# One table of small steps for the attention part, a shift taken off VectorE, and one-hot rows issued by SP alone

## The chip, the core and the metric

The kernel runs on one core of a Trainium2 chip. Five engines run side by side, each through its own list of instructions in order: TensorE (PE in the rows; PEld is its weight load), VectorE (DVE), ScalarE (ACT), GpSimd (POOL) and SyncE (SP). An instruction that has to wait holds up everything behind it on its engine; engines wait for each other through semaphores. SP and ACT also issue DMA transfers (SPq and ACTq in the rows). The metric is the device time of one execution in microseconds (us), as the median of several runs; lower is better.

## The reference

Three blocks in a row: attention restricted to clusters, a soft mixture of experts, and a feed-forward with `h - tanh(h)`.

```python
q_assign = np.argmax(np.einsum('bhsd,hcd->bhsc', q_n, c_n), axis=-1)   # 16 clusters
k_assign = np.argmax(np.einsum('bhsd,hcd->bhsc', k_n, c_n), axis=-1)
mask = q_assign[:, :, :, None] == k_assign[:, :, None, :]
scores = np.where(mask, scale * np.matmul(q, k.transpose(0, 1, 3, 2)), -1e9)
attn = softmax(scores)                      # B=4, H=8, S=768, D=64
x = (attn @ v).transpose(0, 2, 1, 3).reshape(3072, 512)
logits = x @ phi                            # 32 slots
slot_input = softmax_over_tokens(logits).T @ x
slot_out = relu(slot_input @ w1[e]) @ w2[e] # 8 experts, 4 slots each
x = softmax_over_slots(logits) @ slot_out
h = x @ w_in                                # 512 -> 2048; w_in, w_out are float64
out = (h - np.tanh(h)) @ w_out
```

## The kernel before

The attention part works on 16 **pairs** (batch, two heads), numbered p = 0 to 15. For each pair the steps are these functions:

- `load_raw`, `load_v`: q and k (768 KB) and v are loaded. `split_hi` (ScalarE) and `split_lo` (GpSimd) cut q and k into a coarse part and a rest; `xy_hi` and `xy_lo` copy these by DMA into the operand tile `xy`.
- `assign_mm`, `assign_t`, `assign_1` to `assign_6`: the cluster of each token, as one-hot rows. `xy_hot` copies the one-hot rows into `xy` by eight small DMAs, four issued by SP and four by ACT (all eight by SP for p = 0).
- `smax` (18 of them a pair): TensorE makes a row of scores in a PSUM tile `g` (four such tiles), VectorE reduces it to a row maximum `mx`. `sfin_1` to `sfin_4` turn the maxima into one row of `xy` for each head: VectorE, a transpose on TensorE, ScalarE, a DMA out to `row` in DRAM (issued by ACT) and a DMA back into `xy` (issued by SP).
- `st` (24 a pair): two matmuls make scores `st` (two PSUM tiles), ScalarE writes their exponential `E` (six tiles of two heads). `pvmm` (six a pair, kb = 0 to 5) multiplies E by v; GpSimd adds E into the sums `es`, whose single buffer is free again once `fin_sum` of that pair has read it.
- `fin_copy`, `fin_sum`, `fin_ss`, `fin_rec`, `fin_rcp`, `fin_x`, `fin_xm`: sums, division and projection of the pair. There is one `fin_sum` a pair, on TensorE, some six `st` after the pair's last one.
- After the fourth pair of each batch the `fl_` steps compute the batch's slot softmax; most of them are VectorE instructions.

Beside the pairs run 16 conversions of the float64 weights w_in and w_out to float32. Each loads 1 MB (`conv_load`), ScalarE scales the high words (`conv_1`), and VectorE makes the float32 bits from integer words in three passes (`conv_2` shift left, `conv_3` shift right and or, `conv_4` and and or); `conv_8` stores them, `conv_9` sums squares for w_in. `unit` loads 512 KB of expert weights into a buffer as soon as the attention part is done with it; 34 of 80 are issued inside the attention part.

The order in which a step's instructions enter the engine lists is set by a table `PLAN` of due positions: 24 positions are one pair, each step of pair p has one offset for all pairs (a few pairs have their own), all steps are sorted by position, and each step emits all its instructions for all engines at once. So a `smax` puts its matmuls into TensorE's list and its reduction into VectorE's list at the same place of the order, `pvmm` brings its GpSimd additions with it, and `xy_hi`, `xy_lo` and `xy_hot` each bring all their DMAs.

After the attention part come the expert block, paced by its weights, and the feed-forward, neither of which the change touches.

## Time and profile before

| | us |
|---|---|
| time, median of 3 runs | 869.48 |
| lowest and highest | 868.2 and 873.78 |
| the profiled execution, its own time | 873.71 |
| its span in the trace | 871.9 |

The attention part takes the first 514 us of the span, the expert block lasts to about 569 us, and the feed-forward fills the rest. The span is the time from the first to the last instruction; the difference to the execution's own time (1.8 us) is start and end of the program. "PEclk" in the rows is the clock that TensorE was granted, as a share of the full 2.4 GHz (the lower level is 1.2 GHz), averaged over the stretch. A matmul counts as busy also while it is still draining, so a busy TensorE need not be at its peak.

### The profile page before, as it was taken

The numbers are of one execution on the slowest core, as the hardware profiler recorded it, in microseconds if no ns is written. First come the engines' busy times: TensorE is split into PE (matmuls) and PEld (weight loads), VectorE is DVE, ScalarE is ACT, GpSimd is POOL, SyncE is SP. The second block draws the span as 40 slices with busy tenths as digits, with TensorE's granted clock in tenths as the row PEclk, the third lists the DMA queues.
The fourth block names the chain that finished last, engine by engine and source line by source line (L and its number), as shares of the span: only waits on it lengthen the run. The fifth ranks groups of instructions, "written<-read, shape, count | busy, mean of one in ns | idle before, by whom it ended". The sixth has DMA issues, their size and how long they took to land.

```text
span 871.9 us, 12716 instructions
## 1 busy us (share of the span) xinstructions
PE 806.9 (93%) x4327; PEld 541.6 (62%) x4327; DVE 617.7 (71%) x1033; ACT 500.6 (57%) x1069; POOL 403.5 (46%) x235
## 2 busy tenths in 40 slices
PE   1889988999999989999999979989999999999997
PEld 0545554665556556665556543358888888888886
DVE  3577575888768997879986571068767777677774
ACT  3344645565665565556544541179767767677673
POOL 2165975886888778888956741157000000000000
PEclk9988998999999999999999997989999999999999
DMA  6987597668657874777659589970100000000001
GB/s 172 240 217 181 175 215 205 165 175 203 175 164 196 205 191 134 207 197 183 187 156 343 200 320 406 392 292 1 38 25 13 36 1 37 37 0 37 1 38 39
DMA packets 49533, 135.13 MB, mean 155 GB/s; under 512 B 6866, under 2 KB 9350, under 8 KB 49460
## 3 DMA queue, kind: packets, MB, share of 16 engines
q1 hardware_dynamic: 40780, 114.81, 44.9%
q10 hardware_dynamic: 8680, 19.43, 7.2%
q8 instruction: 36, 0.59, 0.3%
q14 instruction: 37, 0.30, 0.1%
HBM read 78.55 MB, written 14.78 MB: 107 GB/s over the span
## 4 chain that ended last, share of the span: by engine, by line
PE 71%; DVE 9%; DMA 3%; ACT 1%; issue 1%; SPq 0%; ACTq 0%; DVEq 0%
PE pv L415 10%; PE acc L1027 10%; PE acc L1025 10%; PE acc L1026 10%; PE g L356 6%; PE st L404 6%; PE st L405 5%; PE u L966 3%; PE h L872 2%; DVE mx L361 2%; PE g L470 2%; PE o L891 2%; PE g L441 1%; DVE pgc L664 1%; DMA xy<-pgb 1%
## 5 line engine op out<-in xcount | busy, mean ns | idle before, releaser
L408 ACT ACTIVATE E<-st 128x384 f32<-128x384 f32 x384 | 168.2, 489 | 184.8 <-PE st L405 141.7
L424 POOL TENSOR_TENSOR es<-es,E 128x768 f32<-128x768 f32 x126 | 252.1, 2020 | 42.4 <-ACT E L408 37.0
L361 DVE TENSOR_REDUCE mx<-g 128x1 f32<-128x512 f32 (+1 forms) x288 | 187.5, 682 | 85.1 <-PE g L356 84.4
L415 PE MATMUL pv<-E,v 128*64 128x384 f32 x768 | 150.8, 513 | 1.9 <-DVE pvc L432 1.9
L1027 PE MATMUL acc<-whi,glo 128*128 128x512 f32 x384 | 150.7, 392 | 0.0
L1025 PE MATMUL acc<-whi,ghi 128*128 128x512 f32 x384 | 150.2, 391 | 0.0
L1026 PE MATMUL acc<-wlo,ghi 128*128 128x512 f32 x384 | 150.0, 391 | 0.0
L404 PE MATMUL st<-xy 112*128 112x384 f32 x384 | 140.8, 367 | 6.4 <-ACT E L408 6.4
L405 PE MATMUL st<-xy 97*128 97x384 f32 x384 | 130.9, 341 | 0.8 <-DMA xy<-row 0.8
L356 PE MATMUL g<-xy 112*128 112x512 f32 (+1 forms) x384 | 117.7, 386 | 9.9 <-DVE mx L361 3.7
L998 DVE TENSOR_TENSOR gt<-u,y 128x384 f32<-128x384 f32 x128 | 71.3, 557 | 50.9 <-ACT y L994 49.7
L356 PEld LDWEIGHTS g<-xy 112*128 112x128 f32 x384 | 67.0, 197 | 62.2 <-issue 16.7
L404 PEld LDWEIGHTS st<-xy 112*128 112x128 f32 x384 | 73.2, 191 | 48.5 <-issue 21.4
L994 ACT ACTIVATE y<-u 128x384 f32<-128x384 f32 x128 | 62.9, 492 | 57.5 <-PE u L966 56.6
L421 POOL TENSOR_TENSOR es<-E 128x768 f32<-128x768 f32 x32 | 58.2, 1841 | 60.3 <-PE g L441 60.3
L415 PEld LDWEIGHTS pv<-E,v 128*64 128x64 f32 x768 | 47.2, 139 | 62.0 <-issue 50.6
L1027 PEld LDWEIGHTS acc<-whi,glo 128*128 128x128 f32 x384 | 72.3, 188 | 17.8 <-DVE glo L1015 2.9
L1025 PEld LDWEIGHTS acc<-whi,ghi 128*128 128x128 f32 x384 | 72.7, 189 | 15.1
L1005 DVE SCALAR_TENSOR_TENSOR gt<-z,gt 128x384 f32<-128x384 f32 x128 | 72.1, 563 | 14.1 <-ACT ghi L1013 0.9
L996 ACT ACTIVATE z<-y,kt 128x384 f32<-128x384 f32 x128 | 79.2, 619 | 4.2
L1026 PEld LDWEIGHTS acc<-wlo,ghi 128*128 128x128 f32 x384 | 72.6, 189 | 10.4
L250 POOL TENSOR_TENSOR pgb<-pga 128x768 fp32r<-128x768 f32 x31 | 61.5, 1986 | 34.8 <-ACT pga L242 23.1
(149 smaller groups left out, 942.2 us busy)
## 6 DMA issues: line engine op xcount, KB each, us to landing
pgw<-in_w_dram SPq DMA_DIRECT2D x64, 512.0 KB
xy<-pga SPq DMA_DIRECT2D x15, 768.0 KB
pga<-in_qk_dram ACTq DMA_DIRECT2D x14, 768.0 KB
pgc<-in_w_in_dram SPq DMA_DIRECT2D x8, 1024.0 KB
pgc<-in_w_out_dram SPq DMA_DIRECT2D x8, 1024.0 KB
xy<-pga SPq DMA_DIRECT2D x18, 384.0 KB
xy<-pga SPq DMA_DIRECT2D x32, 192.0 KB
xy<-pgb SPq DMA_DIRECT2D x32, 192.0 KB
```

Source lines behind the costliest of these rows:

```text
L356: PE.matmul(g[:, o:o + kn], lhsT=x[0:112, QX, qt * 128:(qt + 1) * 128], rhs=x[0:112, KX, k0:k0 + kn], start=True, stop=True)
L361: DVE.tensor_reduce(out=m[:, m0:m0 + w], in_=g.rearrange("p (a b) -> p a b", a=w), axis=AX.X, op=ALU.max)
L404: PE.matmul(s, lhsT=x[0:112, KX, ks], rhs=x[0:112, QX, qs], start=True, stop=False)
L405: PE.matmul(s, lhsT=x[0:97, KY, ks], rhs=x[0:97, QY, qs], start=False, stop=True)
L408: ACT.activation(out=et[p, kb, c][:, h, :], in_=s, func=ACTF.Exp, scale=scale)
L415: PE.matmul(pv[p, c][64 * h:64 * h + 64, :], lhsT=vt[p][:, kb, h, :], rhs=et[p, kb, c][:, h, :], start=(kb == 0), stop=(kb == NKB - 1))
L424: eng.tensor_tensor(out=es[p][:, c], in0=es[p][:, c], in1=e, op=ALU.add)
L996: ACT.activation(out=z, in_=y, func=ACTF.Square, scale=POLY[0], bias=sq_b)
L1005: DVE.scalar_tensor_tensor(out=gt, in0=z, scalar=POLY[2], in1=gt, op0=ALU.add, op1=ALU.mult)
L1025: PE.matmul(acc[t], lhsT=a[:, ts], rhs=whi[:, f, :], start=(f == 0), stop=False)
L1026: PE.matmul(acc[t], lhsT=a[:, ts], rhs=wlo[:, f, :], start=False, stop=False)
L1027: PE.matmul(acc[t], lhsT=l[:, ts], rhs=whi[:, f, :], start=False, stop=(f == KF - 1))
```

## The change

- The table `PLAN` is replaced by `ORDER`. It gives each single step of each single pair its own place, and steps that use several engines are cut into parts with a place each: the matmuls of `smax` and its reduction, the matmuls of `st` and its exponential, the two halves of `fin_copy`, of `setup_2` and of some `fl_` steps. `xy_hi`, `xy_lo`, `xy_rest` and `xy_hot` are cut into single DMAs; the GpSimd additions leave `pvmm` and become steps `es_add`. Functions that have parts are generators, and the emission loop advances them.
- `conv_2`, the left shift on VectorE, is gone. ScalarE makes the low bits instead (`Identity` with a scale and a bias), and `conv_3` shifts left and ors in one VectorE pass. VectorE has two passes for each conversion instead of three, ScalarE two instead of one (three with the squares).
- All eight one-hot DMAs of a pair are issued by SP.

The diff, cut to its core:

```diff
-PLAN = {
-    "A": {
-        "raw": -11.3, "v": 27.0, "hi": [-6.3, -4.2], "lo": [-2.2, 0.1], "mm": 2.1, ...
+ORDER = {
...
+    "xy_hot": (
+        "0,0:26;0,1:27;0,2:25;0,3:23;0,4:57;0,5:30;0,6:35;0,7:33;1,0:116;...
...
     def split_lo(p, h):
-        if h == 0:
+        low(p)
+        (DVE if p == 0 and h == 0 else POOL).tensor_tensor(out=lo[p, h].bitcast(F32R), in0=raw[p, h], in1=hi[p, h], op=ALU.subtract)
...
-    def xy_hot(p):
-        tf = xy[p].bitcast(F32)
-        for h in range(2):
-            for c in range(2):
-                r = 64 * h + 32 * c
-                for a, e in ((QX, SP), (KX, ACT if p else SP)):
-                    e.dma_start(out=tf[96:96 + NC, a, h, c * HS:(c + 1) * HS], in_=oht[p][r:r + NC])
-                    r += NC
+    def xy_hot(p, j):
+        tf = scores(p)
+        h, c, k = j // 4, j // 2 % 2, j % 2
+        r = 64 * h + 32 * c + NC * k
+        SP.dma_start(out=tf[96:96 + NC, KX if k else QX, h, c * HS:(c + 1) * HS], in_=oht[p][r:r + NC])
...
             PE.matmul(g[:, o:o + kn], lhsT=x[0:112, QX, qt * 128:(qt + 1) * 128], rhs=x[0:112, KX, k0:k0 + kn], start=True, stop=True)
             o += kn
+        yield
...
-        for c in range(2):
-            e = et[p, kb, c]
-            if kb == 1:
...
+    def es_add(p, kb, c):
+        if p not in es:
+            es[p] = a1.tile([128, 2, 2, HS], F32, tag="es", name="es")
+        add_engine(p, kb, c).tensor_tensor(out=es[p][:, c], in0=et[p, 0, c] if kb == 1 else es[p][:, c], in1=et[p, kb, c], op=ALU.add)
...
     def conv_2(n):
+        _, lw, sg, _ = cv[n]
+        ACT.activation(out=sg.bitcast(U32), in_=lw.bitcast(U32), func=ACTF.Identity, scale=LO_SCALE, bias=lo_b)
+
+    def conv_3(n):
         hw, _, sg, _ = cv[n]
-        DVE.tensor_scalar(out=sg.bitcast(U32), in0=hw.bitcast(U32), scalar1=3, scalar2=None, op0=ALU.logical_shift_left)
-
-    def conv_3(n):
-        _, lw, sg, _ = cv[n]
         sg = sg.bitcast(U32)
-        DVE.scalar_tensor_tensor(out=sg, in0=lw.bitcast(U32), scalar=29, in1=sg, op0=ALU.logical_shift_right, op1=ALU.bitwise_or)
+        DVE.scalar_tensor_tensor(out=sg, in0=hw.bitcast(U32), scalar=3, in1=sg, op0=ALU.logical_shift_left, op1=ALU.bitwise_or)
...
-    for pos, i, f, a in sorted(ev, key=lambda e: e[:2]):
-        f(*a)
+    todo = sorted((at, k, n, a) for (n, a), ats in order_table().items() for k, at in enumerate(ats))
+    running = {}
+    for _, k, n, a in todo:
+        if k == 0:
+            running[n, a] = named[n](*a)
+        if running[n, a] is not None:
+            next(running[n, a])
```

What this does to the engine lists is seen at three places. The names are tiles: `st` scores, `g` a PSUM tile of `smax` (from `xy`) or of a `fin_` step, `pv` the result of `pvmm`. The line numbers of the two programs differ.

**TensorE, around `fin_sum` of pair 9 (`g<-es`), in the first third of pair 10.** Before:

```order
L356 MATMUL g_3572<-xy_3253 128x512
L415 MATMUL pv_3575<-E_3514,v_3230 64x384 x2
L415 MATMUL pv_3576<-E_3540,v_3230 64x384 x2
L404 MATMUL st_3590<-xy_2910 128x384
L405 MATMUL st_3590<-xy_2910 128x384
L404 MATMUL st_3595<-xy_2910 128x384
L405 MATMUL st_3595<-xy_2910 128x384
L441 MATMUL g_3601<-es_3339,kt_77 32x384 x4
L356 MATMUL g_3610<-xy_3253 128x512
L378 MATMUL g_3613<-kt_77,mxf_3599 6x128
```

After:

```order
L605 MATMUL g_3579<-xy_3149 128x512
L658 MATMUL st_3584<-xy_2848 128x384
L659 MATMUL st_3584<-xy_2848 128x384
L658 MATMUL st_3588<-xy_2848 128x384
L659 MATMUL st_3588<-xy_2848 128x384
L605 MATMUL g_3593<-xy_3149 128x512
L671 MATMUL pv_3596<-E_3503,v_3233 64x384 x2
L671 MATMUL pv_3597<-E_3554,v_3233 64x384 x2
L698 MATMUL g_3606<-es_3291,kt_77 32x384 x4
L671 MATMUL pv_3596<-E_3525,v_3233 64x384 x2
L671 MATMUL pv_3597<-E_3581,v_3233 64x384 x2
L630 MATMUL g_3629<-kt_77,mxf_3622 6x128
```

Before, one `pvmm` stands between every four `st`; now the `pvmm` of kb = 0 and 1 stand together after eight `st`, and so do the others, two by two.

**VectorE, in the first batch's `fl_` steps, from a pair's maximum row on.** (`mx` is a `smax` reduction, `mxf` is `sfin_1`, `xe` is `fin_xm`, `pgc` a conversion; `l`, `lg`, `rm` and `call` belong to the `fl_` steps.) Before:

```order
L366 TENSOR_REDUCE mxf<-mx 128x6
L659 SCALAR_TENSOR_TENSOR pgc<-pgc 128x2x512
L475 TENSOR_TENSOR xe<-g,rr 128x2x256 x2
L495 TENSOR_REDUCE l_1776<-xe 128x192
L497 TENSOR_TENSOR lg<-lg,l_1776 128x192
L505 TENSOR_REDUCE rm<-lg 128x6
L664 SCALAR_TENSOR_TENSOR pgc<-pgc 128x2x512
L361 TENSOR_REDUCE mx<-g 128x1
L509 TENSOR_TENSOR call<-lg,rm 128x192
```

After:

```order
L618 TENSOR_REDUCE mxf<-mx 128x6
L928 SCALAR_TENSOR_TENSOR pgc<-pgc 128x2x512
L732 TENSOR_TENSOR xe<-g,rr 128x2x256
L613 TENSOR_REDUCE mx<-g 128x1
L752 TENSOR_REDUCE l_1832<-xe 128x192
L613 TENSOR_REDUCE mx<-g 128x2
L613 TENSOR_REDUCE mx<-g 128x1 x4
L754 TENSOR_TENSOR lg<-lg,l_1832 128x192
L762 TENSOR_REDUCE rm<-lg 128x6
L688 TENSOR_TENSOR pvc<-pv,pvc 128x384 x2
```

Before, seven VectorE passes stood between two `smax` reductions, two of them conversion passes; now single reductions stand between the batch's steps, and the conversion pass `conv_4` (L928) is done ahead of them.

**SP, around the copies of pair 10's maximum rows (`xy<-row`).** (`xy<-pgb 16x384` are the one-hot rows, `pgc<-in_w_out_dram` a 1 MB `conv_load`, `w_out<-pgc` a `conv_8`.) Before:

```order
L643 DMA pgc<-in_w_out_dram 128x2x512
L320 DMA xy<-pgb 32x1536
L322 DMA xy<-pgb 32x1536
L323 DMA xy<-pgb 64x1536
L324 DMA xy<-onesrow 1x1536
L342 DMA xy<-pgb 16x384 x4
L396 DMA xy<-row 1x768 x2
L676 DMA w_out_75<-pgc 128x2x512
```

After:

```order
L907 DMA pgc<-in_w_out_dram 128x2x512
L594 DMA xy<-pgb 16x384 x7
L650 DMA xy<-row 1x768
L594 DMA xy<-pgb 16x384
L940 DMA w_out_75<-pgc 128x2x512
L907 DMA pgc<-in_w_out_dram 128x2x512
L650 DMA xy<-row 1x768
L562 DMA xy<-pga 64x2x1536
```

Before, both heads' rows followed four one-hot rows together; now the first head's row goes alone behind seven, and the second head's stands last, behind a store and a 1 MB load. By the numbers of the tables, the two heads' copies of pair 10 stand at 1727 and 1755 of the new order and the first `st` that need them at 1757 and 1780, of some 160 places a pair; in `PLAN` the copies stood 2.9 and 7.6 of a pair's 24 positions ahead of the first `st`, which need both.

**SP, in the start of the program.** Before, `load_raw(1)` is followed by all eight one-hot rows of pair 0; now by four of them (head 0), with the rest between other copies. On TensorE the first `smax` of pair 0 stood behind `assign_4(1)`; now it stands ahead of it, behind `assign_mm(1)`.

## Rows read from the trace of the kernel before

**Rows 1.** The page's first part: busy us (share of the span) xinstructions, by engine.

```profile
PE 806.9 (93%) x4327; PEld 541.6 (62%) x4327; DVE 617.7 (71%) x1033; ACT 500.6 (57%) x1069; POOL 403.5 (46%) x235
```

**Rows 2.** Windows: length, busy by engine (xinstructions), PEclk, DMA share, GB/s.

```profile
60.00:150.00 90.00, 80.02 (x415) 47.21 (x412) 60.60 (x90) 46.04 (x104) 60.52 (x31) 0.92 0.75 195
150.00:350.00 200.00, 191.40 (x1099) 117.97 (x1098) 167.31 (x248) 118.74 (x268) 161.55 (x83) 1.00 0.68 181
350.00:410.00 60.00, 59.31 (x345) 36.48 (x343) 52.80 (x79) 34.33 (x76) 50.99 (x26) 1.00 0.75 201
410.00:510.00 100.00, 94.84 (x534) 57.55 (x532) 74.52 (x105) 53.34 (x121) 75.94 (x39) 1.00 0.67 218
```

**Rows 3.** Chain that ended last, `fin_sum` of pairs 2, 8 to 14: start, length, what.

```profile
149.10 0.78 PE g L441 x8
...
325.53 0.78 PE g L441 x8
...
354.83 0.78 PE g L441 x8
...
382.11 0.78 PE g L441 x8
...
409.46 0.78 PE g L441 x8
...
440.12 0.78 PE g L441 x8
...
471.29 0.78 PE g L441 x8
...
496.39 0.78 PE g L441 x8
```

**Rows 4.** Timeline, `fin_sum` of pair 1 on TensorE: start, busy, what.

```profile
113.03 0.85 PE L441 MATMUL g<-es,kt 128*32 128x384 f32 x8
```

**Rows 5.** Timeline of the start: one-hot rows, `assign_mm`, `assign_4`, first `smax`.

```profile
12.45 5.37 SPq L342 DMA_DIRECT2D xy<-pgb  x8
...
17.34 1.51 PE L259 MATMUL g<-pga,cst 128*32 128x384 f32 x8 [6.68 <-DMA pga<-in_qk_dram]
...
21.85 0.50 PE L288 MATMUL g<-hot,first 128*128 128x384 bf16 x1 [3.00 <-DVE hot L283]
...
22.16 5.93 PE L356 MATMUL g<-xy 112*128 112x512 f32 x15
...
23.64 2.58 ACTq L342 DMA_DIRECT2D xy<-pgb  x4
```

**Rows 6.** Chain that ended last, pieces that are no work of TensorE.

```profile
127.79 6.39 DMA xy<-pgb
...
193.66 2.38 DVE pgc L664
...
456.99 3.03 DMA row<-nm
...
460.76 2.94 DMA xy<-row
```

**Rows 7.** Conversion passes by line: xcount: ns min/median/max, first and last start.

```profile
L654 DVE TENSOR_SCALAR pgc<-pgc x16: 684/1239/1670, 59.4 to 490.9; 128x1024 uint32<-128x1024 uint32 x16
...
L664 DVE SCALAR_TENSOR_TENSOR pgc<-pgc x16: 1225/2466/4606, 72.8 to 495.5; 128x1024 uint32<-128x1024 uint32 x16
...
L650 ACT ACTIVATE pgc<-pgc x16: 1124/1150/1177, 49.1 to 489.6; 128x1024 f32<-128x1024 f32 x16
```

**Rows 8.** The page's costliest groups, GpSimd's additions: busy, mean ns of one | idle before.

```profile
L424 POOL TENSOR_TENSOR es<-es,E 128x768 f32<-128x768 f32 x126 | 252.1, 2020 | 42.4 <-ACT E L408 37.0
```

**Rows 9.** Who waited for whom: us in total, times, longest us.

```profile
POOL es L421 <- PE g L441: 60.3, 15, 10.4
```

**Rows 10.** Windows after the attention part, columns as in rows 2.

```profile
510.00:560.00 50.00, 43.10 (x317) 17.48 (x317) 16.40 (x36) 11.94 (x31) 6.71 (x13) 0.86 1.04 394
560.00:580.00 20.00, 15.85 (x153) 8.51 (x146) 8.02 (x27) 9.31 (x23) 4.54 (x5) 0.83 1.05 390
```

More of the change, by code (lines that the diff above doesn't have):

```diff
@@ L82, in _poly, with order_table @@
+def order_table():
+    t = {}
+    for n, rows in ORDER.items():
+        for row in rows.split(";"):
+            a, ats = row.split(":")
+            t[n, tuple(int(x) for x in a.split(",") if x)] = [int(x) for x in ats.split(",")]
+    return t
 def _poly():
@@ L244, in split_lo, with low @@
     def split_lo(p, h):
-        if h == 0:
+        low(p)
+        (DVE if p == 0 and h == 0 else POOL).tensor_tensor(out=lo[p, h].bitcast(F32R), in0=raw[p, h], in1=hi[p, h], op=ALU.subtract)
+    tt = {}
+    def low(p):
+        if (p, 1) not in wp:
             t = r2.tile([128, 4, S], F32, tag="pg", name="pgb")
@@ L249, in split_lo, with scores @@
             tt[p], oht[p] = t[:, 2, 0:HS], t[:, 3, 0:HS]
-        (DVE if PLAN["ev"][1 + h] or (p == 0 and h == 0) else POOL).tensor_tensor(out=lo[p, h].bitcast(F32R), in0=raw[p, h], in1=hi[p, h], op=ALU.subtract)
-    tt = {}
+    def scores(p):
+        if p not in xy:
+            xy[p] = r1.tile([128, 4, 2, S], F32R, tag="pg", name="xy")
+        return xy[p].bitcast(F32)
     def assign_mm(p):
@@ L262, in assign_t @@
     def assign_t(p):
+        low(p)
         DVE.transpose(out=tt[p], in_=asg.pop(p)[:, 0:HS])
@@ L357, in smax @@
             o += kn
+        yield
+        if p not in mxs:
+            mxs[p] = a1.tile([128, 2 * NT, 2], F32, tag="mx", name="mx")
         m = mxs[p].rearrange("p t c -> p (t c)")
@@ L379, in sfin_2, with sfin_3 @@
         fin["g", p, h] = g
-    def sfin_3(p, h):
+    def sfin_3(p, h, c=0):
         if p == 0:
-            for c, g in enumerate(fin.pop(("g", p, h))):
-                ACT.activation(out=xy[p][96:97, QY, h, c * HS:(c + 1) * HS], in_=g[96:97, 0:HS], func=ACTF.Copy, scale=-1.0)
+            ACT.activation(out=xy[p][96:97, QY, h, c * HS:(c + 1) * HS], in_=fin["g", p, h][c][96:97, 0:HS], func=ACTF.Copy, scale=-1.0)
+            yield
             return
@@ L390, in sfin_3 @@
         fin["row", p, h] = row
+        yield
     def sfin_4(p, h):
@@ L776, in tile_cluster_attention_softmoe_ffn @@
-    for n in range(NCV):
-        u = PLAN.get(("V", n), PLAN["V"])
-        v = PLAN["VB"][n]
-        at(v + u["load"], conv_load, n)
-        for i, f in enumerate(CONV):
-            at(v + u["ops"][i], f, n)
-        at(v + u["sq"], conv_9, n)
-        at(v + u["st"], conv_8, n)
-    for x in PLAN["U"]:
-        at(24 * (NPAIR - 2) + x, units, 1)
-    for pos, i, f, a in sorted(ev, key=lambda e: e[:2]):
-        f(*a)
+    fs = (load_raw, load_v, split_hi, split_lo, assign_mm, assign_t, assign_1, assign_2, assign_3, assign_4, assign_5, assign_6, xy_hi, xy_lo, xy_rest,
+          xy_hot, smax, sfin_1, sfin_2, sfin_3, sfin_4, st, pvmm, es_add, fin_copy, fin_sum, fin_ss, fin_rec, fin_rcp, fin_x, fin_xm, fl_lga, fl_lg, fl_r1, fl_l4,
+          fl_r2, fl_tr, fl_tc, fl_r3, fl_cm, fl_ex, fl_r4, fl_et, fl_ec, fl_slot, fl_sc, conv_load, conv_1, conv_2, conv_3, conv_4, conv_9, conv_8,
+          unit, load_rm, setup_2)
@@ L789, in tile_cluster_attention_softmoe_ffn @@
+    named = {f.__name__: f for f in fs}
+    todo = sorted((at, k, n, a) for (n, a), ats in order_table().items() for k, at in enumerate(ats))
[5 more added lines that the diff above has]
+            next(running[n, a])
+    nu[0] = ORDER["unit"].count(":")
     p = NPAIR - 1
-    fin_copy(p, 0)
+    c0, c1 = fin_copy(p, 0), fin_copy(p, 1)
+    next(c0)
     fin_sum(p)
-    fin_copy(p, 1)
+    next(c1)
@@ L793, in tile_cluster_attention_softmoe_ffn @@
+    next(c0)
+    next(c1)
     fin_ss(p)
@@ L814, in tile_cluster_attention_softmoe_ffn @@
     z_al()
-    fl_r2(last)
+    for _ in fl_r2(last):
+        pass
     fl_et(last)
@@ L825, in tile_cluster_attention_softmoe_ffn @@
     fl_slot(last, 1)
-    fl_r3(last)
+    for _ in fl_r3(last):
+        pass
     DVE.scalar_tensor_tensor(out=srun, in0=srun, scalar=fl["al"], in1=fl["gs"], op0=ALU.mult, op1=ALU.add)
```

482 lines of the change are left out of this document (350 added, 132 removed), and 26 rows, old and new, of the table PLAN.

## The prediction, made before any run of the changed kernel

> **What bounds the kernel now.** I read the page's shares first, then the windows, then the chain. TensorE is busy for 93% of the span and VectorE for 71% [rows 1], but the share mixes three stages, and the change touches only the first, some 514 us of attention. In its windows TensorE is busy 191.4 of 200 us from 150 to 350 and 59.3 of 60 from 350 to 410, VectorE 167.3 of 200 and 52.8 of 60, GpSimd 161.6 of 200 [rows 2]: three engines between 80 and 99%, none of which can be left waiting long. What that costs is read from the pace. `fin_sum` runs once a pair, so the distance between two of them on the chain is a pair's time [rows 3]: 27.28 and 27.35 us between 354.83 and 409.46, but 30.66 and 31.17 for the next two, 29.30 before, and 25.10 for pair 14, when there is little left to prepare. From pair 2 to pair 13 it is 322.19 us for eleven pairs, 29.29 on average. So the same work is done at 27.3 us where nothing goes wrong and at 31 where something does, and the chain says what: VectorE, in the pairs with batch work, with a conversion pass of 2.38 us in the middle of it, and transfers of 6.39 and of 3.03 and 2.94 us that TensorE ends up waiting for [rows 6]. An order can win back what lies between the mean and the best pace, not the matmuls themselves.
>
> **The change, part by part.** The sum is made against the profiled execution, 873.71 us, which lies 4.2 us over the median of 869.48; the terms are then taken from the median.
>
> *The shift.* VectorE loses 16 passes of 1.24 us median, 0.68 to 1.67 [rows 7], some 19 us over the attention part, or 1.2 a pair. Its 30 to 31 us pairs are those in which VectorE ends the wait, so there this is worth up to its full 1.2 us, elsewhere less, since TensorE is the bound. ScalarE takes over 16 passes; no row shows this one, but `conv_1` on the same words with the same stride costs 1.15 us [rows 7], 18.4 us in all. ScalarE was busy 118.7 of 200 us [rows 2], which covers it; without cover it would delay an exponential by 1.15 us once a pair. `conv_3` stays one pass of two inputs and I leave its price alone.
>
> *The one-hot rows.* Sixty DMAs go from ACT to SP. Four took 2.58 us of ACT's time [rows 5], in which no exponential could start; that is 39 us off ACT's list, more than the new pass puts on. SP pays 5.37 / 8 = 0.67 us each, 2.7 more a pair. SP issues some 20 DMAs a pair, at this price 13 to 14 us of 27, so it has room, if what it waits for comes in the order of its list; that is the third rival.
>
> *The order.* The largest part. Eleven pairs, 2 to 13, now cost 322.2 us. What the engine lists show is that `st` and `smax` alternate on TensorE, which feeds ScalarE and VectorE evenly; that two `pvmm` stand together, so VectorE and GpSimd can catch up behind a longer stretch of TensorE work; that conversion passes are gone from the middle of the batch work; and that each `xy` DMA is issued by itself. I take as the pace that the old order reached when undisturbed, 27.2 us [rows 3], for the five pairs without batch work, and 28.2 for the six that have it or follow on it, since the batch's own VectorE work still has to go somewhere and only the shift's 1.2 us a pair leaves. That is 5 x 27.2 + 6 x 28.2 = 305.2 us: **-17**. The bounds: no gain at all, if the 27.3 us were already the new order's pace with its own mishaps, to 26.2 us throughout (half way from 27.3 to the 25.1 that pair 14 shows with less work), 288.2 us: -34.
>
> *Pair 2* takes 36.07 us, from 113.03 to 149.10 [rows 3, 4]. It holds the 6.39 us wait for a one-hot copy [rows 6], and TensorE's clock is at 0.92 on average from 60 to 150 [rows 2], part of it at the lower of its two levels. If the copy comes in time, I expect 30: **-6**, between 0 (another copy is late in its place) and -8.
>
> *The start.* The first `smax` began at 22.16 us, right behind `assign_4` of pair 1 at 21.85, which had waited for VectorE [rows 5]. Now it stands behind `assign_mm` of pair 1 alone, which ends at 17.34 + 1.51 = 18.85, and needs four one-hot rows, not eight, that is 4 x 0.67 = 2.7 us less of issuing. But a 1 MB and a 512 KB load now go ahead of pair 0's copies on the same queue. I take **-3**; 0 if these loads hold the copies up by as much, -6 if pair 1 profits too.
>
> *After the attention part* nothing is changed; TensorE's clock there (0.86 from 510 to 560 us) and the full DMA engines (share 1.04 and 1.05) [rows 10] say that weights set its pace, so this stretch moves as a whole: 0 if the weights are requested as much earlier as the attention part ends; that is the second rival.
>
> Sum: -17 - 6 - 3 = -26, so 847.7 for an execution like the profiled one, and 869.5 - 26 = **843.5, I say 844 us**, for the median.
>
> **The rivals.**
>
> *GpSimd sets the pace: 852 us.* A pair has ten additions of 2.02 us [rows 8] and two splits that are as large, 24.2 us, and then GpSimd waits 60.3 / 15 = 4.0 us for `fin_sum` to free the single buffer of sums [rows 9]: 28.2 us a pair, nearly the mean that was measured. If this loop and not the waits of TensorE makes the pace, the new order gains only what a split between the last and the next addition fills of the 4.0 us, and what no longer collides with the shift on VectorE. At 28.2 us for eleven pairs the term is -12, and pair 2's is 0 to -6, so -17 to -18. Against it: pairs of 27.3 us exist with the same GpSimd work.
>
> *The weights take half of it back: 857 us.* If transfers after the attention part are bound by bytes, and their requests hang on buffers that come free no earlier relative to the transfers in front of them, half of the 26 us is waited for at 510 to 580 us. For it: the DMA share there. Against it: the share was 0.67 from 410 to 510 [rows 2], so there was room to request earlier, and the new table puts most `unit` steps a little earlier in the last pairs.
>
> *SP holds the maximum rows up: 895 us.* The second head's row is now the last thing SP issues before a pair, behind eight one-hot rows, a store that waits for VectorE, and often a 1 MB load. On the chain such a row took 2.94 us to come back [rows 6]. If it takes what the late one-hot copy took, 6.39 us, TensorE waits 3.45 us more in each of the 15 pairs that bring their row this way, 52 us, and -26 becomes +26. It decides in favour of slower from 1.7 us a pair on (26 / 15). Against it: the table leaves this copy 25 of some 160 places ahead of the `st` that needs it, about 4 us, which is more than 2.94. The Trainium skill (Perfetto Trace Analysis, DMA Optimizations) speaks against this part of the change: where the issuing of DMAs is the limit, they are better balanced over the engines that can issue them, and here they are taken from two and given to one. By that rule all of SP's added 2.7 us a pair would show, 40 us over 15 pairs, and the sum would be +14; by the rows here SP is not full.
>
> *Nothing changes: 869 us.* TensorE is at 96 to 99% in the long windows [rows 2]; if the slow pairs come from its own pipeline and not from waits, an order moves nothing. Against it: the spread from 27.3 to 31.2 us for the same matmuls.
>
> **How the numbers follow.** The forecast has a chance of 0.58, GpSimd 0.12, the weights 0.10, no change 0.10, slower 0.10. A measurement of this kernel tells about 1% (8.7 us) from no change. Under 860.8 lie the forecast and the first two rivals, 0.79 with a little taken off for the edge of the second (0.78); within 1% lies the fourth with that remainder, 0.12; above it the third, 0.10. The range: at the low end all bounds together give -34 - 8 - 6 = -48, or 821.5, at the high end the range goes up to no change, and leaves out the third rival and the upper half of the fourth: 822 to 870.
>
> **What would show it.** In the profile after, `fin_sum` should stand 27 to 28.5 us apart, with no pair over 30; the first `smax` near 19 us; no transfer over 4 us on the chain before 500 us; VectorE some 19 us less busy, ScalarE some 18 more. The prediction is wrong if the distances stay near 29 with GpSimd or another engine without idle time, if `st` waits for `xy<-row` in most pairs, if the stretch from the last `pvmm` to the first feed-forward matmul grows by what the attention part lost, or if ScalarE's exponentials come late behind the added passes.

## The result, and the profile after

The changed kernel takes 864.27 us (median of 17 runs, 859.87 to 868.52), the kernel before 872.14 in the same series (17 runs): a ratio of 0.991, 95% interval 0.989 to 0.994, so 8 us less. Forecast were 26 less: the direction and the range held, the size did not.

The page's first part of the changed kernel, busy us by engine, beside [rows 1]:

```profile
PE 796.1 (92%) x4327; PEld 543.5 (63%) x4327; DVE 600.5 (69%) x1017; ACT 524.7 (61%) x1085; POOL 396.8 (46%) x235
```

VectorE has 17.2 us less to do and ScalarE 24.1 more. The windows, columns as in [rows 2]:

```profile
60.00:150.00 90.00, 80.79 (x433) 50.20 (x433) 56.64 (x92) 52.62 (x110) 64.64 (x35) 0.94 0.79 207
150.00:350.00 200.00, 195.32 (x1148) 120.70 (x1146) 171.46 (x256) 133.23 (x282) 163.45 (x85) 1.00 0.75 191
...
410.00:510.00 100.00, 94.11 (x537) 58.68 (x535) 69.51 (x100) 58.28 (x127) 70.94 (x37) 0.97 0.69 230
```

From 150 to 350 TensorE is busy 3.9 us longer than before in the same 200, and its clock stays at the upper level. From 410 to 510 the mean clock is 0.97, where it was 1.00 [rows 2]. The chain, `fin_sum` of pairs 1, 2, 3, 13 and 15 (start, length, what), beside [rows 3, 4]:

```profile
125.60 0.83 PE g L698 x8
...
150.58 0.78 PE g L698 x8
...
176.98 0.78 PE g L698 x8
...
463.14 0.78 PE g L698 x8
...
505.59 0.85 PE g L698 x8
```

Pair 1 ends 12.5 us later than before (125.5 against 113.03 [rows 4]), pair 2 1.5 later (150.58 against 149.10 [rows 3]), pair 13 8.2 earlier (463.14 against 471.29) and the whole 7.4 earlier (span 864.5 against 871.9). So the start lost, pair 2 gave nearly all of it back, the eleven pairs from there to pair 13 took 312.56 us instead of 322.19, and what follows the attention part moved as a whole. These are single profiled executions; several of the runs below have one that lies 4 to 9 us off their own median (e3 5.5 above, e8 4.8 and e16 9.1 below), so a difference of a few us between two profiles says little by itself.

The start in the timeline: start, busy, engine, what, and in brackets the idle time before it.

```profile
6.67 0.35 SPq L465 DMA_DIRECT2D xy<-in_rm_dram  x1
...
7.06 0.43 SPq L907 DMA_DIRECT2D pgc<-in_w_in_dram  x1
...
11.82 2.25 SPq L480 DMA_DIRECT2D pga<-in_qk_dram  x1
...
17.86 6.62 SPq L594 DMA_DIRECT2D xy<-pgb  x4
...
25.54 1.51 PE L516 MATMUL g<-pga,cst 128*32 128x384 f32 x8 [14.17 <-DMA pga<-in_qk_dram]
...
26.98 3.87 PE L605 MATMUL g<-xy 112*128 112x256 f32 x10
```

The load of pair 1's raw words is issued at 11.82, as before, but lands at 25.5 instead of 17.3 [rows 5], since 512 KB of `rm` and 1 MB of weights are ahead of it and two loads of v go at the same time (e1 and e2 below move these loads). The first `smax` starts at 26.98 us; the forecast was 18.85. SP itself is held too. Who waited for whom on SP in the first 60 us (total, times, longest):

```profile
SPq L594 <- DMA pga<-in_qk_dram: 4.7, 1, 4.7
SPq L594 <- DMA v<-in_vv_dram: 4.3, 1, 4.3
...
SPq L594 <- DMA pgc<-in_w_in_dram: 3.7, 1, 3.7
```

L594 is `xy_hot`, which has no word of these loads: its issue waits until an earlier transfer has landed, and everything behind it on SP waits with it. The trace shows what it waits for: the kernel's DMAs signal their landing on eight semaphores in turn, and an issue waits until the last transfer that was given the same semaphore has landed. One of these copies, for example, is issued at 23.34, just after a load of v with its semaphore landed at 23.32. So the wait is part of the program.

### The profile page after: what moved, and what is told of

Read it like the earlier page. It is cut to its first block, busy times and chain, and to the rows that moved or that the text cites. A ratio compares the mean times of both kernels' runs of the same rounds, so it can differ in the third digit from the quotient of the medians.

```text
span 864.5 us, 12652 instructions
## 1 busy us (share of the span) xinstructions
PE 796.1 (92%) x4327; PEld 543.5 (63%) x4327; DVE 600.5 (69%) x1017; ACT 524.7 (61%) x1085; POOL 396.8 (46%) x235
## 4 chain that ended last, share of the span: by engine, by line
PE 76%; DMA 9%; DVE 6%; SPq 3%; ACT 2%; issue 1%; POOL 1%; ACTq 0%; DVEq 0%; POOLq 0%
PE pv L671 12%; PE acc L1245 10%; PE acc L1243 10%; PE acc L1244 10%; PE st L658 7%; PE st L659 6%; PE g L605 6%; DMA pga<-in_qk_dram 4%; PE u L1184 3%; PE g L725 2%; PE h L1090 2%; DVE mx L613 2%; PE o L1109 2%; DMA xy<-pga 1%; DMA v<-in_vv_dram 1%
## 5 line engine op out<-in xcount | busy, mean ns | idle before, releaser
L676 POOL TENSOR_TENSOR es<-es,E 128x768 f32<-128x768 f32 x126 | 246.0, 1970 | 43.7 <-ACT E L663 35.8
L663 ACT ACTIVATE E<-st 128x384 f32<-128x384 f32 x384 | 174.9, 490 | 109.6 <-PE st L659 101.6
L613 DVE TENSOR_REDUCE mx<-g 128x1 f32<-128x512 f32 (+1 forms) x288 | 185.0, 682 | 69.4 <-PE g L605 68.4
L658 PE MATMUL st<-xy 112*128 112x384 f32 x384 | 146.9, 383 | 4.3 <-ACT E L663 4.3
L671 PE MATMUL pv<-E,v 128*64 128x384 f32 x768 | 146.3, 505 | 0.0
L605 PE MATMUL g<-xy 112*128 112x256 f32 (+1 forms) x384 | 104.6, 359 | 12.1 <-DMA xy<-pgb 8.5
L605 PEld LDWEIGHTS g<-xy 112*128 112x128 f32 x384 | 69.8, 198 | 23.3 <-issue 11.5
L495 POOL TENSOR_TENSOR pgb<-pga 128x768 fp32r<-128x768 f32 x31 | 58.4, 1889 | 51.6 <-DVE mx L613 24.1
L1223 DVE SCALAR_TENSOR_TENSOR gt<-z,gt 128x384 f32<-128x384 f32 x128 | 71.9, 562 | 13.7 <-ACT ghi L1231 0.5
```

What stands on the lines that cost most here:

```text
L605: PE.matmul(g[:, o:o + kn], lhsT=x[0:112, QX, qt * 128:(qt + 1) * 128], rhs=x[0:112, KX, k0:k0 + kn], start=True, stop=True)
L613: DVE.tensor_reduce(out=m[:, m0:m0 + w], in_=g.rearrange("p (a b) -> p a b", a=w), axis=AX.X, op=ALU.max)
L658: PE.matmul(s, lhsT=x[0:112, KX, ks], rhs=x[0:112, QX, qs], start=True, stop=False)
L663: ACT.activation(out=et[p, kb, c][:, h, :], in_=s, func=ACTF.Exp, scale=scale)
L671: PE.matmul(pv[p, c][64 * h:64 * h + 64, :], lhsT=vt[p][:, kb, h, :], rhs=et[p, kb, c][:, h, :], start=(kb == 0), stop=(kb == NKB - 1))
L676: add_engine(p, kb, c).tensor_tensor(out=es[p][:, c], in0=et[p, 0, c] if kb == 1 else es[p][:, c], in1=et[p, kb, c], op=ALU.add)
```

## The experiments

Each ratio is to the kernel before, run on the same chip in the same series, with its 95% interval. 0.01 is 8.7 us. The changed kernel is 0.991 (0.989 to 0.994). Runs are compared by ratios, since the kernel before itself took 871.27 to 874.19 us in these series.

**The start, four ways.** e1 and e2 add to the table (e2 only the first two lines):

```diff
+    ("conv_load", (0,)): [57.5], ("conv_1", (0,)): [104.5], ("conv_2", (0,)): [112.6], ("conv_3", (0,)): [123.5],
+    ("conv_4", (0,)): [126.5], ("conv_8", (0,)): [136.5], ("conv_9", (0,)): [138.5],
+    ("load_rm", ()): [57.3], ("setup_2", ()): [104.2, 104.4], ("load_v", (0,)): [48.5], ("load_v", (1,)): [126.6],
```

> The changed kernel with its five early loads (1 MB of weights, 512 KB for rmat, 384 KB of v for pairs 0 and 1, with the passes that read them) moved back in the table behind the copies of pair 0; nothing else differs. Theory (the loads ahead of pair 1's raw words and of pair 0's one-hot rows cost the start): pair 1's raw words land near 17.5 us instead of 25.5, the first smax starts at 19 to 20 us instead of 26.98, pair 1's fin_sum at 114 to 119 us instead of 125.5, and the whole is 5 to 9 us shorter than the changed kernel, 855 to 859 us. Rival (the start is slow for another reason: all one-hot rows on one queue, or the new order of smax and st): the first smax moves by less than 3 us and the time by less than 2.

> The changed kernel with only the 1 MB weight load and its passes moved back; the other early loads stay. Theory: of the 2304 KB ahead of pair 1's raw words 1024 are gone, so these land near 21 us instead of 25.5, the first smax starts at 22 to 24 us, and the time is 2 to 5 us shorter, 859 to 862 us. Rival: as in the run with all five loads, under 2 us.

e1: 861.99 us, 0.987 (0.983 to 0.991). e2: 863.42 us, 0.987 (0.982 to 0.992). The timeline of e1:

```profile
17.69 1.51 PE L516 MATMUL g<-pga,cst 128*32 128x384 f32 x8 [6.65 <-DMA pga<-in_qk_dram]
...
19.13 1.22 PE L605 MATMUL g<-xy 112*128 112x256 f32 x3
...
33.74 11.31 SPq L594 DMA_DIRECT2D xy<-pgb  x6
...
44.66 1.50 PE L516 MATMUL g<-pga,cst 128*32 128x384 f32 x8 [6.74 <-DMA pga<-in_qk_dram]
```

The raw words land at 17.7 and the first `smax` starts at 19.13, as the theory said. But pair 1 ended at 121.98 and not at 114 to 119: 7.9 us won at the first `smax` were 3.5 at the end of pair 2 (146.97 against 150.51), and about 3 of the whole (0.987 against 0.991, with intervals that overlap): the next load of raw words, pair 2's, now makes TensorE wait, and six one-hot issues take 11.31 us of SP behind it. In e2, with only the 1 MB load moved, the raw words land at 20.4 and the first `smax` starts at 22.0; its time is not told apart from e1's. Two further kernels go after that wait. e8 puts pair 2's load ahead of the negated maxima and the first weights behind pair 1's copies; e12 is e1 with pair 2's preparation behind the first score tiles:

```diff
+    e8:  ("load_raw", (2,)): [62.5], ("load_rm", ()): [75.5], ("load_v", (0,)): [74.5], ("conv_load", (0,)): [130.5],
+         conv_1 to conv_9 of 0 at 180.5 to 226.5, setup_2 at 110.5 and 110.7
+    e12: ("split_hi", (2, 1)): [143.5], ("split_hi", (2, 0)): [147.5], ("assign_mm", (2,)): [150.5], ("assign_t", (2,)): [151.5],
+         split_lo, assign_1 to 3 and xy_hi of pair 2 at 149.5 to 153.5
```

> The changed kernel with a start in which pair 2's raw words go ahead as well: its load stands ahead of the negated maxima on ACT, rmat and v behind it, the first 1 MB weight load and its passes behind the copies of pair 1. Theory (after the first mending the start still waited 6.9 us for pair 2's raw words, which shared the queue with 1.5 MB): that wait falls under 2 us, pair 2's fin_sum comes at 140 to 145 us instead of 150.51 (146.97 with the first mending), 857 to 861 us. Rival (what is won at the start is given back later in the attention part, at the lower clock or in waits of pair 3): 861 us or more, and the fin_sum of pair 3 no earlier than with the first mending, 174.4 us.

> The first mending of the start (the five loads behind pair 0's copies), and besides pair 2's splits, assignment and copies stand some 20 places later, behind the first eight score tiles of pair 0, which no longer wait for pair 2's raw words. Theory (in the first mending TensorE stood 6.9 us before these words): that wait falls under 2 us, pair 2's fin_sum at 140 to 145 us instead of 146.97, 856 to 860 us. Rival (the start is bound by the transfers themselves, and the wait only moves on to the next of them): no more than 2 us off the first mending, 860 to 864 us.

e8: 865.08 us, 0.993 (0.990 to 0.996); e12: 864.90 us, 0.990 (0.987 to 0.993). Pair 2 ended at 147.56 and 149.35, pair 3 at 173.99 and 175.77. Both expectations failed, and what their rivals say holds, though each misses its own figures a little (pair 3 of e8 is 0.4 us earlier than named, e12 0.9 us above the range named): the wait moves on to the next transfer. Near 50 us TensorE waits 5.15 us in e8 and 9.18 in e12 for one-hot copies, where in e1 it waited 6.74 for raw words and 1.89 for such copies. A start without early loads is worth some 3 us here at best (e1, e2), and nothing to be seen in e8 and e12.

**The shift, in both orders.** e3 is the changed kernel with the shift back, e5 the kernel before with the shift alone moved (its constants added):

```diff
 e3:  conv_2
-        ACT.activation(out=sg.bitcast(U32), in_=lw.bitcast(U32), func=ACTF.Identity, scale=LO_SCALE, bias=lo_b)
+        DVE.tensor_scalar(out=sg.bitcast(U32), in0=hw.bitcast(U32), scalar1=3, scalar2=None, op0=ALU.logical_shift_left)
      conv_3
-        DVE.scalar_tensor_tensor(out=sg, in0=hw.bitcast(U32), scalar=3, in1=sg, op0=ALU.logical_shift_left, op1=ALU.bitwise_or)
+        DVE.scalar_tensor_tensor(out=sg, in0=lw.bitcast(U32), scalar=29, in1=sg, op0=ALU.logical_shift_right, op1=ALU.bitwise_or)
 e5:  the same lines the other way round, in the kernel before
```

> The changed kernel with the left shift back on VectorE and the low bits joined in the second pass as before; order and queues as changed. Theory (VectorE is late in the pairs with batch work, TensorE bounds the rest): VectorE 17 to 20 us busier, ScalarE 18 to 20 us less, eleven pairs 3 to 6 us longer than 312.6, time +3 to +6, 867 to 870 us. Rival (the order made the whole gain): within 1.5 us of the changed kernel.

> The kernel before with only the shift taken from VectorE: ScalarE makes the low bits, VectorE's second pass shifts and joins; order and queues as before. Theory (in the net the shift carries the gain and the new order none): 6 to 10 us shorter than before, 864 to 868 us, and VectorE some 20 us less busy. Rival (the gain needs both, since the old order puts the passes where VectorE is not late): within 3 us of before, 871 to 876 us.

e3: 873.25 us, 0.999 (0.997 to 1.002). e5: 871.63 us, 0.999 (0.996 to 1.003). Neither part gains anything by itself: the rival held in e5, and e3 lost more than its theory said. With both, it is 8 us. `fin_sum` of pairs 3 and 13 in the timelines of before, e5 and e3:

```profile
176.97 0.53 PE L441 MATMUL g<-es,kt 128*32 128x384 f32 x4
...
471.22 0.53 PE L441 MATMUL g<-es,kt 128*32 128x384 f32 x4
```

```profile
174.35 0.53 PE L442 MATMUL g<-es,kt 128*32 128x384 f32 x4
...
468.96 0.53 PE L442 MATMUL g<-es,kt 128*32 128x384 f32 x4
```

```profile
181.98 0.53 PE L698 MATMUL g<-es,kt 128*32 128x384 f32 x4
...
478.76 0.53 PE L698 MATMUL g<-es,kt 128*32 128x384 f32 x4
```

Ten pairs, 4 to 13, take 294.3 us before, 294.6 with the shift alone, 296.8 with the order alone, and 286.2 with both (463.14 - 176.98). The loss of e3 against the changed kernel is not spread over the pairs: pairs 9 and 12 take 33.2 and 36.4 us instead of 28.3 and 29.7, each with a drop of the clock, and the other eight take 1.0 us less in sum. Where the shift's time goes in the old order, the waits tell. Over these ten pairs, VectorE's reductions waiting for the matmuls of `smax` (us in total, times, longest): before, then e5, then the changed kernel, then e3.

```profile
DVE mx L361 <- PE g L356: 43.9, 52, 3.4
```

```profile
DVE mx L362 <- PE g L357: 57.6, 69, 4.7
```

```profile
DVE mx L613 <- PE g L605: 13.6, 26, 1.7
```

```profile
DVE mx L613 <- PE g L605: 12.5, 22, 2.8
```

In the old order VectorE was 12.9 us less busy over these pairs (234.8 against 247.7) and waited 13.7 us longer for TensorE. In the new order only 13.6 us of such waiting are left, which fits that VectorE's work shows there. It is not shown to be the reason: the figure is the same in e3 (12.5) and in e6 below (13.3), whose work of VectorE differs by 45 us over these pairs, and all of VectorE's idle time in them is 46.5 us before and 43.3 in the changed kernel. The passes by line (busy us, mean ns), of the changed kernel and of e3:

```profile
L928 DVE SCALAR_TENSOR_TENSOR pgc<-pgc 128x1024 uint32<-128x1024 uint32 x16 | 32.8, 2047 | 0.0
...
L923 DVE SCALAR_TENSOR_TENSOR pgc<-pgc 128x1024 uint32<-128x1024 uint32 x16 | 30.6, 1914 | 6.3 <-ACT pgc L918 4.1 <-POOL pgb L495 1.5 <-issue 0.4
```

```profile
L928 DVE SCALAR_TENSOR_TENSOR pgc<-pgc 128x1024 uint32<-128x1024 uint32 x16 | 33.3, 2082 | 0.0
...
L923 DVE SCALAR_TENSOR_TENSOR pgc<-pgc 128x1024 uint32<-128x1024 uint32 x16 | 32.9, 2054 | 0.1
...
L918 DVE TENSOR_SCALAR pgc<-pgc 128x1024 uint32<-128x1024 uint32 x16 | 22.3, 1396 | 0.0
```

The shift costs 22.3 us in the new order and makes the pass behind it 2.3 us longer, 25 in all, where I had counted 19.

**The hot rows.** e4 gives ACT half of them back:

```diff
-        SP.dma_start(out=tf[96:96 + NC, KX if k else QX, h, c * HS:(c + 1) * HS], in_=oht[p][r:r + NC])
+        (ACT if p and k else SP).dma_start(out=tf[96:96 + NC, KX if k else QX, h, c * HS:(c + 1) * HS], in_=oht[p][r:r + NC])
```

> The changed kernel with half of the one-hot rows (those of KX, pairs 1 to 15) issued by ACT again, at the same places of the table. Theory (SP has room, ACT too): within 2 us of the changed kernel, 862 to 867 us; ACT then holds exponentials up behind these rows where they wait for an earlier transfer, which makes it 0 to 4 us longer. Rival (SP's list is too long): 4 us or more shorter, with less waiting of st and smax for one-hot rows.

863.73 us, 0.990 (0.987 to 0.993): no difference in the time. The waits did change. What TensorE waits for from 60 us to the end of the attention part (us in total, times, longest): before, then the changed kernel, then e4.

```profile
PE g L356 <- DMA xy<-pgb: 3.5, 1, 3.5
```

```profile
PE g L605 <- DMA xy<-pgb: 6.9, 2, 3.8
PE st L658 <- ACT E L663: 4.3, 11, 1.0
```

```profile
PE st L658 <- ACT E L663: 7.8, 12, 2.1
```

`xy<-pgb` are the one-hot copies. The changed kernel waits for them at 77.6 us (3.82) and at 107.5 (3.12). Every other profile of the new order with all eight on SP waits at these two places too, for these copies or the row of ones issued among them (in e8 the first is 0.75); e4 does not, and ends pair 2 at 145.86 instead of 150.51. Its longer waits for exponentials and a mishap in pair 12 take that back: its ten pairs take 291.0 us. So eight rows on SP do cost waits in the start, four on ACT cost waits for exponentials, and in the sum neither shows.

**Which engine is the bound.** e6 and e10 drop the sign pass in the changed kernel and in e3, e9 in e5; e7 drops two additions a pair:

```diff
 e6, e9, e10:  conv_4
-        DVE.scalar_tensor_tensor(out=sg, in0=hw.bitcast(U32), scalar=0x80000000, in1=sg, op0=ALU.bitwise_and, op1=ALU.bitwise_or)
+        return
 e7:  es_add
+        if kb == 5 and p < NPAIR - 1:
+            return
```

> The changed kernel without the pass that puts the sign bit back (the weights of the feed-forward layer lose their sign): VectorE has 16 passes of 2.05 us, 33 us, less to do, everything else stays. Theory (VectorE is what TensorE waits for in the pairs with batch work, at about 0.4 us of time for each us of VectorE work, as the shift showed with 9 us for 25): 8 to 14 us shorter than the changed kernel, 850 to 856 us. Rival (what is left is TensorE's own work, or the transfers): under 3 us, 861 to 866 us.

> The changed kernel with the shift back on VectorE but without the sign pass (the feed-forward weights lose their sign): VectorE's passes are 16 x (1.40 + 2.05) = 55 us, the changed kernel's 63, the kernel with the shift alone put back 88; ScalarE has no added pass. Theory (the amount of VectorE's work decides in the new order, not which pass it is): as fast as the changed kernel or a little faster, 859 to 866 us. Rival (the shift itself, as the pass that the others wait for, costs): 868 us or more.

> The kernel before with the shift on ScalarE and also without the sign pass (the feed-forward weights lose their sign): VectorE loses another 16 passes of 2.24 us, 36 us, in the old order. Theory (the old order does not wait for VectorE; what it frees goes into waiting for the maxima's matmuls): within 3 us of the old order with the shift on ScalarE, 868 to 874 us. Rival (VectorE bounds the old order too and 20 us were only too little): 5 to 12 us shorter than it, 860 to 867 us.

> The changed kernel without the last two of a pair's ten additions on GpSimd in pairs 0 to 14 (the sums leave out one of six blocks of keys): GpSimd has 30 additions of 1.97 us, 59 us, less to do. Rival of the prediction (GpSimd sets a pace of 28.2 us a pair): 15 us or more shorter, under 850 us. Theory (GpSimd is not the bound, but its additions lengthen VectorE's passes beside them): passes of VectorE 0.1 to 0.3 us shorter on average, 2 to 7 us shorter than the changed kernel, 857 to 862 us. If it only matters as a follower: under 2 us.

e6: 860.33 us, 0.990 (0.985 to 0.995), not told apart from the changed kernel (4 us less by the medians, 1 by the ratios). e10: 865.64 us, 0.992 (0.988 to 0.996), as fast as it. e9: 865.43 us, 0.990 (0.987 to 0.993), while e5 was 0.999. e7: 858.73 us, 0.988 (0.984 to 0.993). So the time does not follow VectorE's work in proportion. In the new order, 25 us more than the changed kernel has lose the whole gain (e3), 7 us less, with the shift in and the sign out, keep it (e10: 33.1 + 23.6 = 56.7 us of passes, 63.4 in the changed kernel), and 33 us less add little or nothing (e6). In the old order 19 us less (598.8 busy, 617.7 before) give nothing, and 52 less (565.9) give 8 us. e6's theory, 0.4 us for each us, falls: it took for a slope what looks like a step. For the new order e10 shows that the amount counts and not which pass it is. For the old order that is open: a slope of 8 us for 52 would give 3 us for 19, which e5's interval still holds and e14's (below) just excludes, and the sign pass of the old order stood in the batch work [rows 6], so its place may count and not its length. GpSimd with 55 us less busy time (342.2, was 396.8) gives 2 to 6 us and not 15: it does not set the pace of 28.2.

**ScalarE's pass.** e11 does it twice; e13 and e14 have it on no engine (e13 in the changed kernel, e14 in e5):

```diff
 e11:  conv_2
+        for _ in range(2):
             ACT.activation(out=sg.bitcast(U32), in_=lw.bitcast(U32), func=ACTF.Identity, scale=LO_SCALE, bias=lo_b)
 e13, e14:  conv_2 returns at once; conv_3
-        DVE.scalar_tensor_tensor(out=sg, in0=hw.bitcast(U32), scalar=3, in1=sg, op0=ALU.logical_shift_left, op1=ALU.bitwise_or)
+        DVE.scalar_tensor_tensor(out=sg, in0=hw.bitcast(U32), scalar=3, in1=lw.bitcast(U32), op0=ALU.logical_shift_left, op1=ALU.bitwise_and)
```

> The changed kernel with ScalarE's new pass done twice: 16 more passes of 1.2 us, 19 us. Theory (ScalarE covers the pass): within 2 us of the changed kernel, 862 to 867 us. Rival (it delays an exponential that TensorE or GpSimd waits for): 5 us or more longer, over 869 us.

> The changed kernel without ScalarE's pass for the low bits; VectorE's second pass keeps its two inputs and takes the low word itself with an and, so the weights of the feed-forward layer are wrong and VectorE's work is the same. Theory (the pass is not covered: done twice it cost 5 us, so once costs 3 to 6): 3 to 6 us shorter than the changed kernel, a ratio to before of 0.984 to 0.988. Rival (ScalarE covers one pass a pair and only a second is too much): within 2 us of the changed kernel, 0.989 to 0.993.

> The kernel before without the shift on VectorE and without the pass on ScalarE, VectorE's second pass with two inputs as in e13 (the weights are wrong). Theory (with the shift on ScalarE the old order gained nothing, because ScalarE's pass took back what VectorE gave): 3 to 6 us shorter than before, a ratio of 0.993 to 0.997 or less. Rival (the old order does not wait for 20 us of VectorE): within 2 us of before, 0.998 to 1.002.

e11: 871.36 us, 0.997 (0.994 to 1.000), 5 us more than the changed kernel: its theory fell. e13: 863.37 us, 0.992 (0.989 to 0.995): one pass a pair costs nothing. e14: 871.03 us, 1.000 (0.997 to 1.004): the old order gains nothing from the shift's absence even where ScalarE does no more. So the first pass is covered and the second is not; where the second one hurts is not traced.

**Without the low bits.** e15 drops conv_2 and makes conv_3 a one-input shift, e16 adds e1's lines:

```diff
 e15, e16:  conv_2 returns at once; conv_3
-        DVE.scalar_tensor_tensor(out=sg, in0=hw.bitcast(U32), scalar=3, in1=sg, op0=ALU.logical_shift_left, op1=ALU.bitwise_or)
+        DVE.tensor_scalar(out=sg, in0=hw.bitcast(U32), scalar1=3, scalar2=None, op0=ALU.logical_shift_left)
```

> The changed kernel without the three low bits of the weights: no pass on ScalarE, and VectorE's second pass is a shift with one input (0.68 us alone instead of 1.2). The weights are cut at 20 bits of mantissa. Theory (VectorE's and ScalarE's work both show): 16 x 0.5 us or more of VectorE less than in e13, 4 to 9 us shorter than the changed kernel, 0.981 to 0.987. Rival (TensorE's own work is what is left): within 2 us of e13.

> As e15, with the five early loads behind pair 0's copies (the first mending of the start). Theory (the start's mending is worth 2 to 3 us beside it): a ratio of 0.978 to 0.985, 2 to 3 us shorter than e15. Rival (what the start gains is given back by pair 2): within 1.5 us of e15.

e15: 858.40 us, 0.988 (0.982 to 0.993). e16: 858.51 us, 0.987 (0.983 to 0.991). Both are ahead of both kernels, of the changed one by 3 us (ratios) to 6 us (medians), with intervals that touch its own; they cut the weights to 20 bits of mantissa. The start's mending again shows little beside it. The profiled execution of e16, at 849.38 us the fastest of its eight, shows the ten pairs from the end of pair 3 on with nothing gone wrong:

```profile
170.06 0.53 PE L698 MATMUL g<-es,kt 128*32 128x384 f32 x4
...
449.02 0.53 PE L698 MATMUL g<-es,kt 128*32 128x384 f32 x4
```

That is 279.0 us for ten pairs. e6, whose profile is at its median and which also had no drop of the clock there, took 279.6 (179.15 to 458.77), e7 280.1, and e1, e8 and e10, without a drop as well, 281.6 to 283.9. The eight profiles of the new order with a drop took 283.6 (e15) to 296.8 (e3).

**What goes wrong in the others.** The changed kernel's TensorE in steps of 10 us (length, busy, clock, DMA share, GB/s):

```profile
420.00:430.00 10.00, 10.00 (x63) 1.00 1.01 262
430.00:440.00 10.00, 7.39 (x42) 0.77 0.93 290
440.00:450.00 10.00, 10.00 (x59) 0.88 0.23 74
450.00:460.00 10.00, 10.00 (x60) 1.00 0.88 295
```

TensorE is idle for 2.6 us, and at the end of that gap the clock falls to its lower level; from 435.5 to 442.3 us its mean is 0.50. Pair 13 takes 32.1 us (430.98 to 463.07), in e1 28.3. What TensorE waited for there is a maximum row (`sfin_1`, L618) from VectorE, in the changed kernel 2.61 us and in e1 0.77:

```profile
436.37 0.37 PE L630 MATMUL g<-kt,mxf 128*6 128x128 f32 x1 [2.61 <-DVE mxf L618]
```

```profile
431.24 0.27 PE L630 MATMUL g<-kt,mxf 128*6 128x128 f32 x1 [0.77 <-DVE mxf L618]
```

VectorE and GpSimd just before, in the changed kernel:

```profile
429.75 1.29 DVE L776 TENSOR_SCALAR rs<-rs 128x6 f32<-128x6 f32 x1
...
432.41 1.66 DVE L784 TENSOR_TENSOR call<-call,rq 128x192 f32<-128x192 f32 x1
```

```profile
429.17 1.85 POOL L495 TENSOR_TENSOR pgb<-pga 128x768 fp32r<-128x768 f32 x1
432.03 3.70 POOL L676 TENSOR_TENSOR es<-E 128x768 f32<-128x768 f32 x2 [1.02 <-PE g L698]
```

And the same two instructions in e1, where no GpSimd pass was under way when they began:

```profile
427.04 0.15 DVE L776 TENSOR_SCALAR rs<-rs 128x6 f32<-128x6 f32 x1
...
428.56 0.35 DVE L784 TENSOR_TENSOR call<-call,rq 128x192 f32<-128x192 f32 x1
```

Six numbers a partition take 0.15 us or 1.29, by whether a GpSimd pass has just begun: it ends at 431.02, and L776 at 431.04. That agrees with the Trainium skill (SBUF — State Buffer, SBUF: two separate sides): the port pair that VectorE and GpSimd share is an exclusive lock for the whole of an instruction, and whoever starts second is blocked until then. In the batch of pairs 12 and 13, L776 and L784 or the subtraction ahead of them, L766, come at such a moment in some kernels and not in others. Where that cost VectorE 2.4 us or more (the changed kernel, e2, e4, e11, e12, e13, e15), TensorE waited 2.4 to 2.6 us for VectorE and a mean clock below 0.87 in a stretch of 10 us follows; where it cost 1.6 or less (e1, e6, e7, e8, e10, e16), TensorE waited 1.1 us at most and the clock stays at 1.00. It is an agreement of thirteen single executions, not an experiment: no run moved these instructions alone. In e3 it is an earlier step of the batch, L754, that takes 5.86 us instead of 0.34; TensorE waits 4.33 us, and the mean clock from 440 to 450 us is 0.69.

## Why the prediction was wrong

Term by term, -17 - 6 - 3 = -26 was forecast, and the profile shows -9.6 for the eleven pairs, +1.5 at the end of pair 2 for everything ahead of them, +0.7 behind them, -7.4 in all. Of the 18.6 us that are missing, 10.5 lie in the start and pair 2, and 7.4 in the eleven pairs.

*The start (-3) and pair 2 (-6): the step that failed.* Together they gave +1.5 instead of -9. I saw that a 1 MB and a 512 KB load go ahead of pair 0's copies and put down 0 as the worst, though the first `smax` hangs on the raw words [rows 5], which took 5.5 us to land (issued at 11.76, used at 17.34). They took 13.7 us behind 2.3 MB, and the first `smax` came 8 us later than forecast. Pair 2's -11.1 (24.98 us instead of 36.07) is not a gain of its own: before, it also paid for a start that was ahead, and for a drop of the clock (0.66 from 130 to 140 us); with the shift alone moved in the old order it took 31.5. The marks of pairs 0 and 1 compare only kernels with the same table, since the new one puts more of the later pairs' work ahead of them; at the end of pair 3 both kernels stand level (176.97 and 176.98). Nor did the wait for a late copy go away, as the -6 assumed. Its size was misread at that: a piece of the chain is the transfer's length, not the wait, and of the 6.39 us TensorE waited 3.53 (of the 3.03 and 2.94 us in pair 13, 0.77). In the changed kernel it waits 6.9 us for such copies, at two places before the end of pair 1, with all eight rows on SP (e4 has neither wait). And mending the start does not bring -9 either: up to 104 us TensorE waits for one transfer after the other, in e1 6.65 and 6.74 us for raw words, then 1.89, 3.80 and 2.78 for copies into `xy`.

*Eleven pairs (-17): mis-sized at -9.6, and the mechanism only half right.* The pace was that of a run in which nothing goes wrong, 278 us for pairs 4 to 13 (305.2 less 27.2 for pair 3). e6 and e16, each with less work for VectorE than the changed kernel, show that the new order can run at 279 to 280. The changed kernel did 286.2. What I took for the order's own merit needs VectorE to be relieved: the order alone gave 296.8, in an execution 5.5 us over its median, and nothing in the whole time (e3). And the mishaps did not go away; at 430 us one alone cost about 4 us, through a clock that had been at 1.00 from 150 to 510 us before [rows 2]. By pairs the forecast was off both ways: the five without batch work took 133.2 us in the changed kernel (27.2 each forecast, 26.6 measured), the six with it 179.4 (28.2 forecast, 29.9 measured), and in four of these six TensorE is idle for 0.6 us or less. The kernel before already showed this: its pair 5 took 29.3 us without any idle time. Pair 5 before, then pairs 5 and 13 of the changed kernel, as windows of TensorE (length, busy, clock, DMA share, GB/s):

```profile
207.15:236.47 29.32, 29.32 (x177) 1.00 0.66 173
```

```profile
206.61:236.66 30.05, 29.68 (x182) 1.00 0.84 218
...
430.98:463.07 32.09, 29.48 (x168) 0.89 0.70 235
```

I had not counted that the batch brings matmuls of its own (L789, L820, L834), which no order removes: 0.8 to 1.1 us of TensorE in the first pair of each batch's work and 2.3 in the second. Over the eleven pairs together, before and after:

```profile
149.03:471.22 322.19, 308.83 (x1771) 1.00 0.69 188
```

```profile
150.51:463.07 312.56, 304.34 (x1772) 0.99 0.74 195
```

TensorE was idle for only 13.4 us of them, so -17 asked for more than all of its waiting. Of the 9.6 us that were won, 5.1 are idle time (8.2 are left) and 4.5 busy time, which counts a matmul's draining too; why that shrank is not traced.

*The shift.* Its worth was forecast at up to 1.2 us in the slow pairs; taken back it cost 8 us, the whole gain, in the profile through two pairs with gaps and drops of the clock and not evenly. In the old order it is worth nothing. Its price on ScalarE was rightly nothing (e13), but the cover is thin (e11).

*The one-hot rows* at no gain and no loss: right in the time (e4), but partly by luck, since two costs that the forecast did not have cancel: waits for the copies in the start with all eight on SP, waits for exponentials with four on ACT. The 40 us that the prediction worked out by the balancing rule did not come.

*Behind the attention part* 0: right; from the last `fin_sum` to the end it is 358.3 us before (871.9 - 513.6) and 358.9 after. *The rivals:* GpSimd as the pace fell (e7), the weights took nothing back, the maximum rows were not late in every pair (TensorE never waits over 0.15 us for one in the changed kernel from 60 us on). "Nothing changes" (869) came closest in time and the weights' rival (12.5 less) closest as a difference, both by luck: neither names what happened. The chances of the forecast and the first two rivals add up to 0.80, not 0.79; nothing hangs on it. Of the signs named, the first `smax` near 19 us, no pair over 30 us (pair 13 took 32.1) and no transfer over 4 us on the chain (9.10 and 10.56 at 260 and 310 us) failed.

What stays open is which transfer order would let the first pairs start without waits, why the relief of VectorE counts in the new order and not in the old one, and what the second pass on ScalarE delays.

## What to carry to other kernels

Undo each part of a change in both surroundings before crediting it: here the order and the shift were worth nothing each and 8 us together. Neither the busy share of VectorE nor its total of idle time (46.5 and 43.3 us of ten pairs) would have told that. Bytes that are put ahead of the first tile's operands delay the head of the kernel, here by 8 us, so the bound of such a step has to reach into the loss; what moving them back brings at the end is another matter (3 us here). And a pace read from the best pairs is the pace without mishaps; the new order did not remove the chance meetings of VectorE and GpSimd, and in the changed kernel the gap that one of them made in TensorE's work was paid again in its clock.
